# Mode parameters in two halves, low parts of the weights on VectorE, integers of phases on TensorE

## The chip, the cores and the metric

The kernel runs on one core of a Trainium2 chip. Its engines are TensorE (PE, with weight loads PEld), VectorE (DVE), ScalarE (ACT), GpSimd (POOL) and SyncE (SP), which issues nearly all the transfers. The metric is the device time of one execution in microseconds.

## The reference

A sequence `u` of 2048 positions and 448 channels goes through two branches, mixed by a gate for each position:

```python
g = _sigmoid((x * gate_w).sum(-1, keepdims=True))
a = _A_ref(x, ...)      # S4D convolution + skip
b = _B_ref(x, ...)      # (sigmoid(x W) * (x V)) W2, with 1792 inner features
return g * a + (1 - g) * b

# _A_ref: 448 channels, 256 modes each
A = -jnp.exp(log_A_real) + 1j * A_imag
C = (C_real + 1j * C_imag) * dt[:, None]
P = jnp.exp((A * dt[:, None])[:, :, None] * pos[None, None, :])
K = 2.0 * jnp.einsum("dn,dnl->dl", C, P).real
y = irfft(rfft(u_t, 2 * L) * rfft(K, 2 * L))[:, :, :L]
```

All is fp32.

## The kernel before

Four pieces of work share the engines.

- **Parameters** (`params`, tiles of the pool `pro`). From 448 x 256 mode parameters DVE, ACT and POOL make the phases of the modes in turns (each split into a high and a low part, `hi` and `lo`, stored to the DRAM tensor `phd`) and powers of their decays (`bsx`, stored to `bsd`). ACT takes exp, tanh, arctan and sin for it and loads a table at each change between these. The step size `dtv` is computed for 4 columns of 112 channels; its way to all 128 partitions (`dtb`) is a store to DRAM (`dtd`) and a load with broadcast.
- **Mode generation** (`kgen`, 28 chunks of 16 channels, 14 to each half of the channels). Chunk `c` loads its phases `ph` and powers `bs`, POOL multiplies the powers up to a table `tb` (`powers`), and for each half of the modes (`half_chunk`, so 56 of them) there are two calls of `turns`, each for 512 columns: PE multiplies phases with positions into PSUM (`tp`, L973), the integer is taken off, and ACT takes sine and cosine (`fr`, `ec`). DVE multiplies these with products of `tb` (`es`, `ec`: L1012, L1026, L1028, L1030, L1032; a half chunk has six such products), and PE sums over the modes into `kp` (L1038). After 14 chunks half of the convolution kernel K goes to the DRAM tensor `kd`.
- **Transforms** (`Chain`): `spectrum_u` for both halves of `u`, beside mode generation; then for each half the transform of K, the product with the spectrum of `u`, and the way back to the output. They need `kd`.
- **GLU** (`glu_w`, `glu_up`, `glu_down`, `glu_end`): 2 halves of the positions x 14 tiles of features. Each fp32 operand is split into a high part (`wh`, `vh`, `xs`, `hh`, cast by ACT) and a low part (`wl`, `vl`, `hl`, the difference), and each product is three fp32r matmuls: `gu` into 512 columns (L1142 to L1147), `dn` into 448 (L1159 to L1161). DVE does `sg`, `hl` and `ob` (L1131, L1134, L1175).

The integer of a phase comes off in one of two ways. In the half chunks that `PEM = (1, 2)` puts on PE, ACT rounds twice (L983 and L984, which leaves minus the integer in `nn`), PE repeats the product and adds `nn` by an identity matrix (L988), and ACT reads PSUM (L990, L991). In the others ACT rounds once (L978), DVE subtracts (L979), and ACT goes on from SBUF (L1002, L1003). With `(1, 2)` every second half chunk goes either way.

The low parts of the weights are computed in `glu_split`, L1118. Where the group (7 for each half of the positions) is under `GLO = 12` POOL does it, else DVE.

No order is written out. Every operation is recorded with its engine, a cost and a priority; `Plan.order` runs them through a model of the machine (`Clock`) and starts, on the engine that is free first, the ready operation of lowest priority number. `RANK` overwrites priorities by engine, tile and stage. The order found is fixed in the program, so each engine waits in that order. Buffers are counted per tile name (`tp` 2, `nn` 1, `kp` 1, `gu` 2, `dn` 1, `tb` 2), and a pool can be opened when the pools in its `after` have no work left: `eg` (mode generation) and `fu` (the first transforms) both follow `pro`, in which also the gate's and GLU's first inputs lie (`gt`, `xr0`).

Of the kernel before, what the change touches and what calls it, by code (L numbers as in the profile page):

```python
# [28 lines left out]
    ('Act', 'ec', 20): (-63, -6.5, 45, 54.5, 20, 20, 20, 20),  # L29
    ('Act', 'ex0', 10): -65.5,  # L30
    ('Act', 'fr', 20): (20, 20, 20, 20, 20, 41, -4.5, -4.5),
    ('Act', 'fx', 30): 110.5,
    ('Act', 'fx', 40): 91.5,
    ('Act', 'hh', 21): (21, 36, 36, 36, -17.5, 21),
    ('Act', 'hh', 45): 53.5,
    ('Act', 'ke', 20): -130.5,
    ('Act', 'nn', 20): (20, 20, 51, 51, 60, -97.5, 20, 20),
    ('Act', 'ob', 21): (-15.5, 21),
    ('Act', 'sg', 5): (5, 5, 125.5, 125.5, 5),
    ('Act', 'sg', 21): (21, 21, 68, 68, 68, -73.5),  # L40
    ('Act', 'sg', 45): 34.5,
    ('Act', 'th0', 10): -24,
    ('Act', 'vh', 5): -148,
    ('Act', 'vh', 21): (80, 61, 21),
    ('Act', 'wh', 5): -110,
    ('Act', 'wh', 21): (-131, 17, 21, 21, 21, 21),
    ('Act', 'xs', 5): -122.5,
    ('DVE', 'aci', 10): -43.5,
    ('DVE', 'dtp', 10): 0.5,
    ('DVE', 'dtv', 10): -76.5,  # L50
# [145 lines left out]
class Pool:  # L196
    def __init__(self, plan, name, space, after, below):
        self.plan, self.name, self.space, self.after, self.below = plan, name, space, after, below
        self.stack, self.tp = ExitStack(), None
# [9 lines left out]
    def real_pool(self):  # L209
        if self.tp is None:  # L210
            for p in self.after:
                p.stack.close()
            if self.below is not None:
                self.below.real_pool()
            self.tp = self.stack.enter_context(self.plan.tc.tile_pool(
                name=self.name, bufs=1, **({} if self.space is None else dict(space=self.space))))
# [1070 lines left out]
```

## Time and profile before

| | |
|---|---|
| time, median of 3 runs | 800.59 us (798.03 to 802.04) |
| profiled execution | 799.93 us, of which 797.8 us span |
| mean granted TensorE clock | 0.966 |
| busy: PE, DVE, ACT, POOL | 736.6, 714.9, 491.9, 342.0 us |
| HBM traffic | 74.39 MB read, 36.24 MB written, 139 GB/s over the span |

How to read a row of the groups: line, engine, operation, written tile `<-` read tiles, shapes, count | busy us, mean ns of one | idle time of the engine just before these instructions, and what ended most of it. Durations overlap a little: the next instruction of an engine can start before the last one's end, so prices are better taken from start to start. A timeline row begins with start and length in us. Matmuls overlap most.

### The profile page before, as it was taken

To read this page: it belongs to the slowest core of one execution; us is meant where nothing else is said; L and a number is where in the kernel's file an instruction comes from. 1 tells how busy PE (TensorE), PEld (TensorE's weight loads), DVE (VectorE), ACT (ScalarE), POOL (GpSimd) and SP (SyncE) were. 2 spreads that over 40 slices of the span, in tenths; PEclk is the share of its full clock that TensorE was granted. 3 is DMA by queue.
4 is the path that set the end of the run, shared out by engine and by line. 5 is a ranking of instruction groups with operands and counts; after the bars stand their busy time and mean duration, and the time that the engine had idled before them with its cause. 6 is when DMAs were issued, how large, how long until landed. Compare 5 with 4: busy or idle time off the path is not lost.

```text
span 797.8 us, 16605 instructions
## 1 busy us (share of the span) xinstructions
PE 736.6 (92%) x6688; PEld 526.8 (66%) x6688; DVE 714.9 (90%) x910; ACT 491.9 (62%) x818; POOL 342.0 (43%) x342
## 2 busy tenths in 40 slices
...
GB/s 284 195 108 70 175 191 202 149 185 200 74 115 185 136 117 210 166 242 139 170 137 183 239 71 12 43 12 51 30 73 256 209 38 99 117 109 131 204 102 173
DMA packets 97940, 111.71 MB, mean 140 GB/s; under 512 B 31272, under 2 KB 84840, under 8 KB 97352
## 3 DMA queue, kind: packets, MB, share of 16 engines
...
q8 instruction: 53, 0.87, 0.5%
q0 software_dynamic: 256, 0.46, 0.2%
...
HBM read 74.39 MB, written 36.24 MB: 139 GB/s over the span
## 4 chain that ended last, share of the span: by engine, by line
PE 47%; DVE 29%; ACT 7%; DMA 5%; issue 5%; POOL 3%; SPq 2%; DVEq 0%; ACTq 0%; POOLq 0%
PE gu_gps L1142 5%; PE gu_gps L1144 5%; PE gu_gps L1143 5%; PE kp_egp L1038 4%; PE dn_gps L1159 4%; PE fps_fups L617 4%; DVE ec_eg L1030 3%; PE dn_gps L1160 3%; DVE es_eg L1012 3%; PE dn_gps L1161 3%; PE tp_egp L973 3%; DVE es_eg L1032 2%; SPq L484 2%; DMA kd<-ke_eg 2%; DMA vr_glu<-in_w_dram 2%
## 5 line engine op out<-in xcount | busy, mean ns | idle before, releaser
L1142 PE MATMUL gu_gps<-xs_glu,wh_glu 128*128 128x512 f32 x336 | 141.2, 420 | 18.7 <-ACT wh_glu L1116 10.8
L1143 PE MATMUL gu_gps<-xs_glu,wh_glu 128*128 128x512 f32 x336 | 134.5, 400 | 0.0
L1144 PE MATMUL gu_gps<-xs_glu,wl_glu 128*128 128x512 f32 x336 | 134.2, 399 | 0.2 <-POOL wl_glu L1118 0.2
L1012 DVE TENSOR_TENSOR es_eg<-tb_eg 128x1024 f32<-128x1024 f32 (+1 forms) x112 | 118.1, 1079 | 2.8 <-PE kp_egp L1038 1.9
L1159 PE MATMUL dn_gps<-vh_glu,hh_glu 128*128 128x448 f32 x224 | 90.8, 405 | 7.5 <-DVE ob_glu L1175 4.3
L1142 PEld LDWEIGHTS gu_gps<-xs_glu,wh_glu 128*128 128x128 f32 x336 | 64.9, 193 | 40.8 <-ACT wh_glu L1116 10.8
L959 POOL TENSOR_TENSOR tb_eg<-tb_eg 128x96 f32<-128x96 f32 (+2 forms) x84 | 88.1, 1054 | 5.6
L1160 PE MATMUL dn_gps<-vh_glu,hl_glu 128*128 128x448 f32 x224 | 83.3, 372 | 4.3 <-DVE hl_glu L1134 4.3
L1161 PE MATMUL dn_gps<-vl_glu,hh_glu 128*128 128x448 f32 x224 | 82.9, 370 | 1.1 <-POOL vl_glu L1118 1.1
L1118 POOL TENSOR_TENSOR wl_glu<-xr_glu,wh_glu 128x512 fp32r<-128x512 f32 x44 | 73.2, 1676 | 24.9 <-ACT wh_glu L1116 24.9
L973 PE MATMUL tp_egp<-pos_sb,ph_eg 96*128 96x512 f32 x168 | 73.7, 458 | 9.3 <-DVE fr_eg L979 5.4
L1032 DVE TENSOR_TENSOR es_eg<-fr_eg,es_eg 128x1024 f32<-128x1024 f32 x56 | 81.7, 1459 | 0.1
L1118 POOL TENSOR_TENSOR vl_glu<-vr_glu,vh_glu 128x448 fp32r<-128x448 f32 x24 | 36.0, 1500 | 103.9 <-ACT vh_glu L1116 102.1
L1030 DVE TENSOR_TENSOR ec_eg<-ec_eg,es_eg 128x1024 f32<-128x1024 f32 x56 | 76.5, 1365 | 0.1
L1144 PEld LDWEIGHTS gu_gps<-xs_glu,wl_glu 128*128 128x128 f32 x336 | 64.8, 193 | 15.9 <-POOL wl_glu L1118 0.9
L1143 PEld LDWEIGHTS gu_gps<-xs_glu,wh_glu 128*128 128x128 f32 x336 | 65.1, 194 | 11.5 <-issue 0.4
L1130 ACT ACTIVATE sg_glu<-gu_gps 128x512 f32<-128x512 f32 x56 | 33.5, 598 | 55.4 <-PE gu_gps L1147 52.4
L949 POOL MEMSET tb_eg<- 128x96 f32 x28 | 7.8, 285 | 134.3 <-DVE es_eg L1012 133.5
L1005 ACT ACTIVATE ec_eg<-ec_eg,half_pi 128x1024 f32<-128x1024 f32 x56 | 64.5, 1151 | 0.5
L1159 PEld LDWEIGHTS dn_gps<-vh_glu,hh_glu 128*128 128x128 f32 x224 | 42.4, 189 | 31.1 <-issue 8.1
L1175 DVE SCALAR_TENSOR_TENSOR ob_glu<-dn_gps,og,ob_glu 128x448 f32<-128x448 f32 x72 | 48.5, 673 | 9.7 <-PE dn_gps L1161 9.2
L1133 ACT ACTIVATE hh_glu<-sg_glu 128x512 fp32r<-128x512 f32 x56 | 34.4, 629 | 36.8 <-DVE sg_glu L1131 33.4
...
## 6 DMA issues: line engine op xcount, KB each, us to landing
...
```

Of the source, the lines that this page charges most:

```text
L959: pool(96 * m, lambda n=n, m=m: G.tensor_mul(g3(n + 1, m), g3(1, m), g3(n, 1).to_broadcast([128, 32, 3, m])))
L973: T.matmul(tp.real, ph[:, c % 2, 128 * nh:128 * nh + 128].bitcast(F32R), pos[:, 512 * i:512 * i + 512], start=True, stop=last)
L1012: V.tensor_mul(o.rearrange("p d (i k) -> p d i k", k=ny), x.unsqueeze(3).to_broadcast([128, 16, nx, ny]), y.unsqueeze(2).to_broadcast([128 ...
L1030: op("DVE", c_dve(1024), lambda: V.tensor_mul(ec[:, :, 32:96], ec[:, :, 32:96], es[:, :, 32:96]), [(es, 1), (es, 2)], [(ec, "p")], prio)
L1032: op("DVE", c_dve(1024), lambda: V.tensor_mul(es[:, :, 32:96], fr.real, es[:, :, 32:96]), [fr], [(es, 1), (es, 2)], prio)
L1118: op(eng, cost(n), lambda: e.tensor_sub(view(l), a(), view(h).bitcast(F32)), [res, (h, key)], [(l, key)], prio)
L1142: T.matmul(p.real, wh[:, k, cs], x[:, k], start=(k == 0), stop=False)
L1143: T.matmul(p.real, wh[:, k, cs], x[:, 4 + k], start=False, stop=False)
L1144: T.matmul(p.real, wl[:, k, cs], x[:, k], start=False, stop=False)
L1159: T.matmul(p[:, :D], hh[:, ts], vh.real, start=(i == 0), stop=False)
L1160: T.matmul(p[:, :D], hl[:, ts], vh.real, start=False, stop=False)
L1161: T.matmul(p[:, :D], hh[:, ts], vl.real, start=False, stop=(i == len(fs) - 1))
```

## The change

- `params` runs once for each half of the channels (`g` = 0, 1), on half as many columns, with its own loads, stores and table loads. `phd` and `bsd` are tracked by half, so chunks 0 to 13 need the first half alone. The second half has the priority `P_PRO1 = 19`, one ahead of mode generation's 20.
- The step sizes are computed once (`step_sizes`). A diagonal matrix of them, multiplied on PE by a matrix of ones, spreads them over the partitions in PSUM; `dtd` is gone.
- `GLO = 0`: the low parts of all weights are computed on DVE. POOL did 24 of 28 tiles of features before (two `wl` and one `vl` each).
- `PEM = (1, 1)`: in all 56 half chunks the integer comes off on PE; L979, L978, L1002 and L1003 are no longer issued.
- The pool `pro` is divided: gate and first GLU inputs are in `pre` on one side of SBUF, and `eg` follows `pre` there; `pro` and after it `fu` lie on the other side.
- `RANK` is another table of priorities throughout.

```diff
-    ('DVE', 'wl', 45): 272,
+    ('DVE', 'wl', 21): 109.5,
+    ('DVE', 'wl', 45): 123,
...
-PEM = (1, 2)
-GLO = 12
+PEM = (1, 1)
+GLO = 0
...
-P_PRO, P_E, P_U, P_K, P_G, P_GV = 10, 20, 30, 40, 60, 21
+P_PRO, P_PRO1, P_E, P_U, P_K, P_G, P_GV = 10, 19, 20, 30, 40, 60, 21
...
-    pro, fups = plan.pool("pro"), plan.pool("fups", PSUM)
-    fu = plan.pool("fu", after=[pro])
-    eg, egp = plan.pool("eg", after=[pro], below=fu), plan.pool("egp", PSUM)
+    pre, fups = plan.pool("pre"), plan.pool("fups", PSUM)
+    pro = plan.pool("pro", side="right")
+    fu = plan.pool("fu", after=[pro], side="right")
+    eg, egp = plan.pool("eg", after=[pre]), plan.pool("egp", PSUM)
...
+        ones = pro.tile("ones", 1, (P, 128))
+        op("DVE", c_fast(128), lambda: V.memset(ones.real, 1.0), [], [ones], prio)
+        return dt2, dtp, dtv, ones
+
+    def params(g, sizes, prio):
+
+        dt2, dtp, dtv, ones = sizes
...
+        W, Q, cols, raw = 2 * N, D, slice(2 * g, 2 * g + 2), {}
...
-            for z, y in ((0, hi), (1, lo)):
-                dma(lambda z=z: phd[kind + z].rearrange("(t p) n -> p t n", p=P), lambda y=y: y.real.bitcast(F32),
-                    P * W * 4, [y], [(phd, kind + z)], prio)
-        dma(lambda: dtd.v("t p -> p t"), dtv, P * 16, [dtv.res], [dtd], prio, 0.35)
...
+        diag, dtb = pro.tile("diag", 1, (P, 2, P)), fups.tile("fps", FPS, (128, 512))
+        for i in range(2):
+            op("DVE", c_fast(P), lambda i=i: V.tensor_scalar(
+                diag[:, i], idn[0:P, 0:P].bitcast(F32), dtv()[:, 2 * g + i:2 * g + i + 1], None, op0=ALU.mult),
+               [idn, dtv.res], [(diag, i)], prio)
+        op("PE", c_mm4(HD), lambda: T.matmul(dtb[:, :HD], ones.real, diag.v("p t q -> p (t q)"), start=True, stop=True),
+           [ones, diag], [dtb], prio)
...
                 dma(lambda i=i: ph[:, i], lambda i=i: phd[:, 16 * (c + i):16 * (c + i) + 16], 96 * 1024,
-                    [phd], [(ph, i)], prio, 115.0)
+                    [(phd, (k, c // 14)) for k in range(6)], [(ph, i)], prio, 115.0)
...
-    params(P_PRO)
+    sizes = step_sizes(P_PRO)
+    params(0, sizes, P_PRO)
     gate(2, P_G2)
     gate(3, P_G2)
+    params(1, sizes, P_PRO1)
     kgen_consts(P_E)
```

What the new priorities make of the order shows at three places. Line numbers after the change are higher by 31 or 32 for the same statement (L1012 becomes L1043, L1118 becomes L1150).

First, DVE at the start of mode generation: before, from the last parameter operation (`bsx`) to the first product `es`.

```order
L893 TENSOR_TENSOR bsx_pro_971<-th_pro_807,ex_pro_802 128x2x14x32
L1175 SCALAR_TENSOR_TENSOR ob_glu_624<-dn_gps_962,og,ob_glu_624 128x448
L1131 SCALAR_TENSOR_TENSOR sg_glu_954<-sg_glu_954,gu_gps_950 128x512
L1134 TENSOR_TENSOR hl_glu_1006<-sg_glu_898,hh_glu_996 128x512
L1175 SCALAR_TENSOR_TENSOR ob_glu_678<-dn_gps_983,og,ob_glu_678 128x448
L1134 TENSOR_TENSOR hl_glu_1026<-sg_glu_954,hh_glu_1000 128x512
L1131 SCALAR_TENSOR_TENSOR sg_glu_1046<-sg_glu_1046,gu_gps_1040 128x512
L1134 TENSOR_TENSOR hl_glu_1089<-sg_glu_1046,hh_glu_1082 128x512
L1012 TENSOR_TENSOR es_eg_1138<-tb_eg_1055 128x16x64
```

And after, up to the first `es`:

```order
L924 TENSOR_TENSOR bsx_pro_1260<-th_pro_1178,ex_pro_1189 128x2x7x32
L834 TENSOR_TENSOR lo_pro_1266<-acr_pro_761,hi_pro_1228 112x512
L1150 TENSOR_TENSOR wl_glu_1272<-xr_glu_826,wh_glu_1244 128x512
L1150 TENSOR_TENSOR wl_glu_1272<-xr_glu_885,wh_glu_1244 128x512
L1150 TENSOR_TENSOR vl_glu_1313<-vr_glu_1255,vh_glu_1304 128x448
L1163 SCALAR_TENSOR_TENSOR sg_glu_1284<-sg_glu_1284,gu_gps_1276 128x512
L1150 TENSOR_TENSOR wl_glu_1334<-xr_glu_888,wh_glu_1315 128x512
L1207 SCALAR_TENSOR_TENSOR ob_glu_491<-dn_gps_1166,og,ob_glu_491 128x448
L1150 TENSOR_TENSOR wl_glu_1334<-xr_glu_1195,wh_glu_1315 128x512
L834 TENSOR_TENSOR lo_pro_1353<-mx_pro_820,hi_pro_1292 112x512
L1043 TENSOR_TENSOR es_eg_1379<-tb_eg_1274 128x16x64
```

The parameters' operations (here the second half's) now reach up to the first `es`, and low parts of weights stand among them: 22 `wl` and 8 `vl` are ahead of the first `es` on DVE, 24 and 12 between it and the last one, 10 and 8 behind.

Second, DVE within the first chunk: before, from the middle of the first half chunk to the end of the second.

```order
L1030 TENSOR_TENSOR ec_eg_1160<-ec_eg_1160,es_eg_1138 128x16x64
L1175 SCALAR_TENSOR_TENSOR ob_glu_467<-dn_gps_1202,og,ob_glu_467 128x448
L979 SCALAR_TENSOR_TENSOR fr_eg_1190<-fr_eg_1190,tp_egp_1212 128x512
L1028 SCALAR_TENSOR_TENSOR es_eg_1138<-fr_eg_1119,es_eg_1138 128x16x32
L1032 TENSOR_TENSOR es_eg_1138<-fr_eg_1119,es_eg_1138 128x16x64
L1026 TENSOR_TENSOR ec_eg_1265<-ec_eg_1265,es_eg_1171 128x16x32
L1030 TENSOR_TENSOR ec_eg_1265<-ec_eg_1265,es_eg_1171 128x16x64
```

After, the same stretch:

```order
L1061 TENSOR_TENSOR ec_eg_1370<-ec_eg_1370,es_eg_1379 128x16x64
L1059 SCALAR_TENSOR_TENSOR es_eg_1379<-fr_eg_1332,es_eg_1379 128x16x32
L1063 TENSOR_TENSOR es_eg_1379<-fr_eg_1332,es_eg_1379 128x16x64
L1166 TENSOR_TENSOR hl_glu_1491<-sg_glu_1146,hh_glu_1479 128x512
L1057 TENSOR_TENSOR ec_eg_1443<-ec_eg_1443,es_eg_1403 128x16x32
L1166 TENSOR_TENSOR hl_glu_1529<-sg_glu_1215,hh_glu_1517 128x512
L1207 SCALAR_TENSOR_TENSOR ob_glu_561<-dn_gps_1450,og,ob_glu_561 128x448
L1166 TENSOR_TENSOR hl_glu_1541<-sg_glu_1284,hh_glu_1531 128x512
L1061 TENSOR_TENSOR ec_eg_1443<-ec_eg_1443,es_eg_1403 128x16x64
```

The subtraction L979, which stood between the products, is gone; GLU's operations still stand there.

Third, PE in the first chunk: before, the first product of the second half chunk (`tp_egp_1179`, whose integer DVE subtracts, as it does that of `tp_egp_1212` above), and the end of the first half chunk's second call of `turns` (`tp_egp_1115`).

```order
L973 MATMUL tp_egp_1179<-pos_sb,ph_eg_1034 128x512
L973 MATMUL tp_egp_1115<-pos_sb,ph_eg_1034 128x512
L988 MATMUL tp_egp_1115<-nn_eg_1173,idn 128x512
L1142 MATMUL gu_gps_1162<-xs_glu_166,wh_glu_720 128x512
L1143 MATMUL gu_gps_1162<-xs_glu_166,wh_glu_720 128x512
```

After, the ends of the two calls of `turns` for the second half chunk (`tp_egp_1387` and `tp_egp_1399`).

```order
L1004 MATMUL tp_egp_1387<-pos_sb,ph_eg_1223 128x512
L1019 MATMUL tp_egp_1387<-nn_eg_1413,idn 128x512
L1174 MATMUL gu_gps_1394<-xs_glu_115,wh_glu_1170 128x512
L1175 MATMUL gu_gps_1394<-xs_glu_115,wh_glu_1170 128x512
L1176 MATMUL gu_gps_1394<-xs_glu_115,wl_glu_1186 128x512
L1174 MATMUL gu_gps_1394<-xs_glu_115,wh_glu_1170 128x512
L1175 MATMUL gu_gps_1394<-xs_glu_115,wh_glu_1170 128x512
L1176 MATMUL gu_gps_1394<-xs_glu_115,wl_glu_1186 128x512
L1004 MATMUL tp_egp_1399<-pos_sb,ph_eg_1223 128x512
L1019 MATMUL tp_egp_1399<-nn_eg_1436,idn 128x512
L1191 MATMUL dn_gps_1450<-vh_glu_1099,hh_glu_1106 128x448
```

The pair of a repeated `tp` and its `nn` now comes for every call of `turns`: 224 + 112 matmuls into `tp` in place of 168 + 56. Between the first and the last `kp` PE has 555 `gu` and 312 `dn` in place of 611 and 324, and behind the last `kp` 305 and 210 in place of 302 and 210. SP issues 31 transfers for the parameters in place of 18.

More of the change, by code (lines that the diff above doesn't have):

```diff
@@ L28 @@
 RANK = {
[L29 to L50, printed above, removed]
[23 rows of a table removed]
-    ('DVE', 'uax', 40): (-66, 40),
-    ('DVE', 'ubx', 40): 55,
[31 rows of a table removed]
+    ('Act', 'acr', 10): 271,
+    ('Act', 'ci', 10): 33,
+    ('Act', 'cr', 10): 123.5,
+    ('Act', 'dots', 2): 39,
+    ('Act', 'ec', 20): (20, -161.5, 24.5, 24.5, 20, -7, -7, 30),
+    ('Act', 'ex0', 10): -38,
+    ('Act', 'ex1', 10): 195.5,
+    ('Act', 'fr', 20): (20, 20, 20, 20, 38.5, 38.5, 31, 31),
+    ('Act', 'fx', 30): 168.5,
+    ('Act', 'fx', 40): (40, 40, 40, -20, -20, -20, -20, -20),
+    ('Act', 'hh', 21): -5,
+    ('Act', 'hh', 45): 167.5,
+    ('Act', 'ke', 20): (89.5, 89.5, 20, -26.5, 20, -19.5, 20, 20),
+    ('Act', 'nn', 20): (-125, -125, -125, -6, 20, -179, 31, 20),
+    ('Act', 'ob', 5): 153,
+    ('Act', 'ob', 21): -110.5,
+    ('Act', 'rt', 19): 47.5,
+    ('Act', 'sg', 5): (5, 13, 198, 198, 5),
+    ('Act', 'sg', 21): (21, 21, 21, 174.5, 174.5, 174.5),
+    ('Act', 'sg', 45): 55.5,
+    ('Act', 'th1', 10): 105.5,
+    ('Act', 'th1', 19): -42,
+    ('Act', 'vh', 21): (21, 145.5, -19.5),
+    ('Act', 'vh', 45): -108,
+    ('Act', 'wh', 21): (-35, -35, -35, 111, 111, 111),
+    ('Act', 'wh', 45): 84,
+    ('DVE', 'acr', 19): 116.5,
[29 rows of a table added]
+    ('DVE', 'uax', 40): -207,
+    ('DVE', 'ubx', 40): 226.5,
[33 rows of a table added]
 }
@@ L212, in real_pool @@
                 p.stack.close()
[L213 to L216, printed above, removed]
+            kw = {} if self.space is None else dict(space=self.space)
+            if self.side is not None:
+                kw["side"] = self.side
+            self.tp = self.stack.enter_context(self.plan.tc.tile_pool(name=self.name, bufs=1, **kw))
         return self.tp
@@ L299, in __init__, with pool @@
         self.tc, self.ops = tc, []
-    def pool(self, name, space=None, after=(), below=None):
-        return Pool(self, name, space, after, below)
+    def pool(self, name, space=None, after=(), side=None):
+        return Pool(self, name, space, after, side)
     def op(self, eng, cost, fn, r=(), w=(), prio=0, after=(), size=0, table=None):
@@ new lines, in gated_mix, with __init__, __call__, rw @@
+    class A:
+        def __init__(self, res, f=lambda r: r):
+            self.res, self.f = res, f
+        def __call__(self):
+            return self.f(self.res.real)
+    def rw(o, *ins):
+        return [x.res for x in ins], [o.res]
+    P = 112
+    steps, POW = (64.0, 1.0, 512.0, 8.0), (2, 0, 3, 1)
+    class Params:
+        def __init__(self, prio):
+            self.prio = prio
+        def ts(self, o, a, s1, s2, o0, o1=None, n=2 * N):
+            kw = dict(op0=o0) if o1 is None else dict(op0=o0, op1=o1)
+            op("DVE", c_fast(n), lambda: V.tensor_scalar(o(), a(), s1, s2, **kw), *rw(o, a), self.prio)
+        def stt(self, o, a, s, b, o0, o1, n=2 * N):
+            op("DVE", c_dve(n), lambda: V.scalar_tensor_tensor(o(), a(), s, b(), op0=o0, op1=o1), *rw(o, a, b), self.prio)
+        def tt(self, o, a, b, o0, n=2 * N):
+            op("DVE", c_dve(n), lambda: V.tensor_tensor(o(), a(), b(), op=o0), *rw(o, a, b), self.prio)
+        def act(self, o, a, fn, n=2 * N, table=None, **kw):
+            op("Act", c_act(n), lambda: S.activation(o(), a(), fn, **kw), *rw(o, a), self.prio, table=table)
+        def mk(self, name, w=(2, N), dt=F32, rows=P):
+            return A(pro.tile(name, 1, (rows, *w), dt))
@@ L874, in params @@
         split(mx, 2)
-        bsx = pro.tile("bsx0", 1, (128, 14, 2, 32))
-        for nh in halves:
-            amp_t(cr, idn, bsx, nh, prio)
-        bs_store(bsx, 4, prio)
+        bsx = pro.tile("bsx0", 1, (128, 7, 2, 32))
+        for nh in range(2):
+            amp_t(cr, bsx, nh, prio)
+        bs_store(bsx, 4, g, prio)
         for i in range(4):
```

136 lines of the change are left out of this document (59 added, 77 removed), and 113 rows, old and new, of the table RANK.

## The prediction

> **What bounds the kernel now.** I read the page's engine shares first, then the chain, then the same busy times cut into the three stages of the program.
>
> ```profile
> PE 736.6 (92%) x6688; PEld 526.8 (66%) x6688; DVE 714.9 (90%) x910; ACT 491.9 (62%) x818; POOL 342.0 (43%) x342
> ...
> PE 47%; DVE 29%; ACT 7%; DMA 5%; issue 5%; POOL 3%; SPq 2%; DVEq 0%; ACTq 0%; POOLq 0%
> ```
>
> TensorE (PE) and VectorE (DVE) are both full, and the chain of work that ended last changes between them. The stages are cut at the first `es` product (129.3 us, timeline below) and at the last one, which starts at 584.75 and lasts 1.23.
>
> ```profile
> 0.00:129.30 129.30, 105.99 (x440) 85.19 (x441) 104.28 (x143) 68.98 (x107) 65.41 (x51) 0.96 0.67 171
> 129.30:586.00 456.70, 430.17 (x5200) 309.46 (x5198) 437.06 (x490) 369.59 (x614) 269.49 (x286) 0.96 0.46 130
> 586.00:797.80 211.80, 200.45 (x1058) 132.13 (x1050) 173.60 (x279) 53.37 (x97) 7.14 (x6) 0.99 0.55 142
> ```
>
> Columns: stretch, length, then busy PE, PEld, DVE, ACT, POOL, granted clock, DMA. In stage 2 (mode generation with GLU work between) DVE is busy 437.1 of 456.7 us, 95.7%; PE 94%. But a busy PE has slack that busy time does not show:
>
> ```profile
> 559.00 0.50 PE L973 MATMUL tp_egp<-pos_sb,ph_eg 96*128 96x512 f32 x1
> 559.34 0.40 PE L1146 MATMUL gu_gps<-xs_glu,wh_glu 128*128 128x512 f32 x1
> 559.58 0.39 PE L1147 MATMUL gu_gps<-xs_glu,wl_glu 128*128 128x512 f32 x1
> ```
>
> A matmul of 512 columns counts 0.40 busy, yet the next starts 0.24 later, and 0.34 behind the one of 96 rows; a `dn` of 448 columns I take at 0.2. So DVE bounds stage 2, with PE close behind.
>
> **The parts, stage by stage.** Counts come from the two programs' orders, durations from this execution.
>
> *Stage 3 first.* Behind the last mode product PE has 302 `gu` and 210 `dn` matmuls left before the change, 305 and 210 after, and the same transforms. DVE gets 2 `wl` and 4 `vl` more, some 3.3 us where it is busy 82%. I take +1, so everything hangs on when stage 2 ends.
>
> *Low parts from POOL to DVE.*
>
> ```profile
> L1118 POOL TENSOR_TENSOR wl_glu<-xr_glu,wh_glu 128x512 fp32r<-128x512 f32 x44 | 73.2, 1676 | 24.9 <-ACT wh_glu L1116 24.9
> L1118 POOL TENSOR_TENSOR vl_glu<-vr_glu,vh_glu 128x448 fp32r<-128x448 f32 x24 | 36.0, 1500 | 103.9 <-ACT vh_glu L1116 102.1
> L1118 DVE TENSOR_TENSOR wl_glu<-xr_glu,wh_glu 128x512 fp32r<-128x512 f32 x8 | 5.4, 691 | 0.1
> L1118 DVE TENSOR_TENSOR vl_glu<-vr_glu,vh_glu 128x448 fp32r<-128x448 f32 x4 | 2.5, 614 | 0.0
> 558.26 0.69 DVE L979 SCALAR_TENSOR_TENSOR fr_eg<-fr_eg,tp_egp 128x512 f32<-128x512 f32 x1
> 558.87 0.68 DVE L1028 SCALAR_TENSOR_TENSOR es_eg<-fr_eg,es_eg 128x512 f32<-128x512 f32 x1
> 579.32 1.21 DVE L1030 TENSOR_TENSOR ec_eg<-ec_eg,es_eg 128x1024 f32<-128x1024 f32 x1
> 580.45 0.67 DVE L1175 SCALAR_TENSOR_TENSOR ob_glu<-dn_gps,og,ob_glu 128x448 f32<-128x448 f32 x1
> ```
>
> The last four rows are neighbours in the timeline: a DVE operation of 512 elements takes 0.61 from start to start, one of 1024 takes 1.13, so 1.0 ns an element and 0.08 fixed. A `wl` is 0.61, a `vl` of 448 about 0.54. Stage 1 gets 22 and 8 of them (17.7 us), stage 2 gets 24 and 12 (21.1 us). What queues behind them on DVE are the mode products, for which PE waits.
>
> *Integers taken off on TensorE.* The 56 operations of L979 go from DVE: 56 x 0.61 = 34.2 us, all in stage 2. They also stood in a loop with two waits, which go with them; their place is taken by the loop over `nn`, which half of the chunks have already:
>
> ```profile
> ACT ec_eg L1002 <- DVE fr_eg L979: 21.9, 16, 4.3
> DVE ec_eg L1026 <- ACT ec_eg L1005: 11.0, 12, 3.1
> PEld tp_egp L973 <- DVE fr_eg L979: 9.3, 13, 3.5
> PEld tp_egp L988 <- ACT nn_eg L984: 5.5, 11, 1.5
> ```
>
> (engine, line, whom it waited for: us in total, times, longest.) The `nn` wait doubles, +5.5; up to 9.3 goes. I cost the two as nothing; the cover is GLU matmuls standing between, and in 460 to 540 us, where these are few, the wait is bare.
>
> PE gains 56 repeated L973 and 56 L988. In stage 2 that is 109 matmuls, 26 us by 0.24 or 37 by 0.34; out of stage 2 into stage 1 go 56 `gu` and 12 `dn`, 15.8 us; 8 transform matmuls come in, 2 us. Net +12 to +23; I take 12, since most of the added ones follow a neighbour of 128 rows.
>
> ACT gets, for each of 28 half chunks, twice (L983, L984, L990, L991) instead of twice L978, L1002 and L1003:
>
> ```profile
> L984 ACT ACTIVATE nn_eg<-fr_eg 128x512 fp32r<-128x512 f32 x56 | 35.6, 637 | 0.1
> L991 ACT ACTIVATE fr_eg<-tp_egp 128x512 f32<-128x512 f32 x56 | 33.7, 601 | 11.2 <-PE tp_egp L988 10.9
> L990 ACT ACTIVATE ec_eg<-tp_egp 128x512 f32<-128x512 f32 x56 | 33.6, 601 | 6.1 <-PE tp_egp L988 6.0
> L978 ACT ACTIVATE fr_eg<-tp_egp 128x512 f32<-128x512 f32 x56 | 32.1, 610 | 8.8 <-DVE es_eg L1032 8.8
> L983 ACT ACTIVATE fr_eg<-tp_egp 128x512 f32<-128x512 f32 x56 | 30.7, 591 | 3.7 <-DVE es_eg L1032 1.8 <-PE tp_egp L973 1.3 <-DMA ph_eg<-phd 0.3
> L1002 ACT ACTIVATE ec_eg<-fr_eg 128x1024 f32<-128x1024 f32 x28 | 29.7, 1060 | 22.2 <-DVE fr_eg L979 21.9
> L1003 ACT ACTIVATE fr_eg<-fr_eg 128x1024 f32<-128x1024 f32 x28 | 29.5, 1053 | 0.3
> ```
>
> That is 4.86 against 3.33 us: +43 us on 369.6, less 5 for nine GLU casts and sigmoids that went to stage 1. It stays under a 436 us stage (94% at most, since neighbours overlap): costed at nothing, covered by DVE and PE. If those got faster still, ACT would be next.
>
> *Contention between POOL and DVE.*
>
> ```profile
> L1032 DVE TENSOR_TENSOR es_eg<-fr_eg,es_eg x56: 1208/1220/2332, 143.9 to 584.8; 128x1024 f32<-128x1024 f32 x56
> L1032 DVE TENSOR_TENSOR es_eg<-fr_eg,es_eg 128x1024 f32<-128x1024 f32 x56 | 81.7, 1459 | 0.1
> L1030 DVE TENSOR_TENSOR ec_eg<-ec_eg,es_eg 128x1024 f32<-128x1024 f32 x56 | 76.5, 1365 | 0.1
> L979 DVE SCALAR_TENSOR_TENSOR fr_eg<-fr_eg,tp_egp 128x512 f32<-128x512 f32 x56 | 37.7, 678 | 2.3 <-ACT fr_eg L978 2.0
> 129.30:586.00 456.70, 0.00 (x0) 71.37 (x43) 0.96 0.46 130
> 129.30:586.00 456.70, 118.08 (x112) 200.23 (x243) 0.96 0.46 130
> ```
>
> L1032 takes 1220 in the median but 1459 in the mean; L1030 1365. Against 1220 that is 13.4 and 8.1 us, and the whole stretch lies between these 21.5 and about 50 over all products on SBUF operands. L979, which reads PSUM, is not stretched (678). The last two rows are POOL's busy time in stage 2 on L1118 and on `tb`: 71.4 and 200.2. By that share, 26% of 50, the low parts' leaving gives 13 us. Ends: 0, if `tb` meets the same products anyway, and 50. I take 13, the share that the rows show.
>
> [...]
>
> *Stage 2's sum.* DVE: 437.1 - 34.2 + 21.1 - 2.4 (three `sg`, one `ob` fewer) - 13 = 408.6; at the same 95.7% the stage would last 427. PE: 430.2 + 12 = 442 busy. In the last 46 us before 586 both engines are full at once (45.70 and 45.93):
>
> ```profile
> 460.00:540.00 80.00, 68.19 (x865) 48.64 (x864) 77.00 (x82) 63.01 (x101) 51.50 (x56) 0.87 0.11 31
> 540.00:586.00 46.00, 45.70 (x547) 35.11 (x545) 45.93 (x53) 31.36 (x49) 17.63 (x15) 1.00 0.11 36
> ```
>
> So neither has to give way, but PE cannot go far under 442/0.99 = 446 except by the 0.17 us tails that fill gaps. Between 427 and 446 I take 436: -21 us.
>
> *Halves and step sizes, stage 1.*
>
> ```profile
> 116.51 1.08 DVE L893 TENSOR_TENSOR bsx_pro<-th_pro,ex_pro 128x896 f32<-128x896 f32 x1
> ...
> 126.32 0.69 DVE L1131 SCALAR_TENSOR_TENSOR sg_glu<-sg_glu,gu_gps 128x512 f32<-128x512 f32 x1 [3.55 <-PE gu_gps L1147]
> ...
> 129.29 1.88 DVE L1012 TENSOR_TENSOR es_eg<-tb_eg 128x1024 f32<-128x1024 f32 x1 [0.77 <-POOL tb_eg L959]
> ...
> 0.00:129.30 129.30, 0.00 (x0) 35.76 (x23) 0.96 0.67 171
> ...
> L832 ACT ACT_TABLE_LOAD x2 | 2.6, 1283 | 0.0
> ```
>
> (The row with 35.76 is POOL's busy time on L1118 in stage 1.) Parameters end at 117.6; store, load and powers take until 129.3, and DVE stands idle for some 6 of these 11.7 us, 3.55 in one piece. After the change the second half of the parameters fills that gap, since the loads for chunk 0 need the first half alone. But in the order every one of the second half's DVE rows still stands before the first `es`, with 30 low parts: halving moves no parameter work behind the start. DVE: 104.3 + 17.7 + 3 (35 split operations by 0.08) + 2.4 (three `sg`, one `ob`) = 127.4, less a relief at stage 2's price for POOL's time, 13/71.4 of 35.8: 6.5 (ends 0 and 25, from 0 and 50 there). The idle 25 falls by the gap's 6 at least; I take 8 for it. Sum 121 + 17 = 138, of which I keep 137: +8. It isn't lost: 53 `gu` and 12 `dn` have been done by then. ACT's six more table loads, 1.28 us each, are covered by its idle 60 us. SP's 13 more parameter transfers move the same bytes: nothing, between 0 and the gap's 6. The step sizes' trip through DRAM goes, one matmul per half comes: nothing, since `la` then waits for DVE's own queue.
>
> [...]
>
> **Sum.** 137 + 436 + 213 = 786 of span against 797.8; the execution took 799.93, 2.1 more, and lies 0.08% under the median of 800.59. I predict 788.
>
> **Rivals.** *PE bounds (slower).* PE keeps the waits that it has, at 94% busy, and the 109 added matmuls come on top at 0.34 in place of 0.24: stage 2 becomes 456.7 + 23 = 480, or 469 at the low price; with +8 and +1 the run takes 832 or 821, less what the waits for L979 gave (9.3), so 812 at the least. Against: 12 of PE's 26.5 idle us lie in 460 to 540, where DVE is 96% busy. It decides from the point where stage 2 needs over 448 us. 812.
>
> *Traded evenly.* No relief from POOL, and products wait for ACT's longer loop (the 11.0 us of L1026 double): DVE 421.6 + 11 and 456.7 - 437.1 idle give 452, or 441 without the doubled wait; with 137 + 213 + 2 that is 804 or 793, in the middle 799.
>
> *More comes.* Relief 26, twice its share, and both engines full: DVE 396/0.97 = 408, PE at its 0.24 pitch not in the way; stage 1 unchanged. 129 + 408 + 213 + 2 = 752 at most; half of the way from the forecast, 770.
>
> **How the numbers follow.** The forecast has 0.5, more comes 0.2, traded evenly 0.17, PE bounds 0.13. Within 0.5% means within 4 us of 800.6, about what a measurement tells from no change. Faster holds the first two: 0.70; same 0.17; slower 0.13. The range cuts the lower half of "more comes" and the upper half of "PE bounds": 771 to 812. The forecast's own range is 779 to 796.
>
> **What would show it.** Right: first `es` at 135 to 139, last one at 565 to 580; DVE busy in between near 409; means of the two 1024-element products under 1400; POOL near 230 in all; the waits for L979 gone. Wrong: PE over 97% busy in stage 2 with DVE under 90%; products waiting for ACT above 20 us; a first `es` before 125, if parameters by halves start the modes early after all; or a stage 3 off 212 by over 4.

## The result, and the profile after

The changed kernel takes 778.32 us (median of 4 runs, 777.54 to 781.98) against 800.58 us (798.03 to 802.04) in runs on the same chip: a ratio of 0.9734, 95% interval 0.9695 to 0.9774, so 22 us less. The profiled execution after has a span of 776.4 us.

The page's engine shares and granted clock after:

```profile
PE 743.2 (96%) x6804; PEld 539.9 (70%) x6804; DVE 687.8 (89%) x967; ACT 527.3 (68%) x962; POOL 230.4 (30%) x282
...
PEclk9999999999999999999999999999999999999999
```

PE works 6.6 us more than before, and the span is 21.4 shorter: PE's idle time fell from 61.2 to 33.2 us. The windows say where, cut as before at the first and the last `es` product (length, then busy PE, PEld, DVE, ACT, POOL, granted clock, DMA):

```profile
0.00:136.20 136.20, 119.79 (x519) 97.98 (x520) 114.50 (x218) 87.90 (x154) 39.41 (x46) 0.99 0.62 168
136.20:560.30 424.10, 419.84 (x5234) 307.68 (x5233) 397.36 (x467) 386.77 (x712) 190.94 (x237) 1.00 0.52 138
560.30:776.40 216.10, 203.53 (x1054) 134.25 (x1053) 175.97 (x285) 52.62 (x97) 0.00 (x0) 0.99 0.54 139
```

Against 129.3, 456.7 and 211.8: stage 1 is 6.9 longer, stage 2 32.6 shorter, stage 3 4.3 longer. PE's idle time in stage 2 went from 26.5 to 4.3 us, and the stretch 460 to 540, where PE had worked 68.19 of 80 at a clock of 0.87, is full:

```profile
460.00:540.00 80.00, 79.84 (x928) 61.16 (x928) 76.63 (x91) 71.64 (x130) 34.02 (x45) 1.00 0.15 49
```

The groups of DVE's products and of its new low parts:

```profile
L1063 DVE TENSOR_TENSOR es_eg<-fr_eg,es_eg 128x1024 f32<-128x1024 f32 x56 | 72.6, 1297 | 0.1
L1061 DVE TENSOR_TENSOR ec_eg<-ec_eg,es_eg 128x1024 f32<-128x1024 f32 x56 | 71.2, 1272 | 0.5
L1043 DVE TENSOR_TENSOR es_eg<-tb_eg 128x1024 f32<-128x1024 f32 x56 | 69.7, 1245 | 10.2 <-PE kp_egp L1069 6.0 <-POOL tb_eg L993 1.6 <-POOL tb_eg L990 1.3
L1150 DVE TENSOR_TENSOR wl_glu<-xr_glu,wh_glu 128x512 fp32r<-128x512 f32 x52 | 37.1, 735 | 1.2 <-ACT wh_glu L1148 1.2
```

The means of the first two were 1459 and 1365. The waits that the prediction spoke of (whole span: us, times, longest):

```profile
ACT ec_eg L1021 <- PE tp_egp L1019: 15.1, 19, 3.9
DVE ec_eg L1057 <- ACT ec_eg L1036: 12.1, 13, 2.9
DVE vl_glu L1150 <- ACT vh_glu L1148: 12.0, 5, 5.1
PEld tp_egp L1019 <- ACT nn_eg L1015: 2.4, 8, 0.8
```

Those for L979 are gone. The wait of PE's weight loads for `nn`, expected to double from 5.5, fell to 2.4; a matmul of GLU now stands right in front of 73 of the 112 repeated products (29 of 56 before). New is DVE's wait for the cast `vh`.

### The profile page after: what moved, and what is told of

Its sections match the earlier page's. It is cut to its first block, busy times and chain, and to the rows that moved or that the text cites. A ratio compares the mean times of both kernels' runs of the same rounds, so it can differ in the third digit from the quotient of the medians.

```text
span 776.4 us, 17036 instructions
## 1 busy us (share of the span) xinstructions
PE 743.2 (96%) x6804; PEld 539.9 (70%) x6804; DVE 687.8 (89%) x967; ACT 527.3 (68%) x962; POOL 230.4 (30%) x282
## 5 line engine op out<-in xcount | busy, mean ns | idle before, releaser
L1174 PE MATMUL gu_gps<-xs_glu,wh_glu 128*128 128x512 f32 x336 | 136.3, 406 | 11.2 <-ACT wh_glu L1148 10.8
L1175 PE MATMUL gu_gps<-xs_glu,wh_glu 128*128 128x512 f32 x336 | 132.6, 394 | 0.0
L1043 DVE TENSOR_TENSOR es_eg<-tb_eg 128x1024 f32<-128x1024 f32 x112 | 107.8, 987 | 10.2 <-PE kp_egp L1069 6.0
L1004 PE MATMUL tp_egp<-pos_sb,ph_eg 96*128 96x512 f32 x224 | 97.1, 440 | 0.6 <-ACT fr_eg L1014 0.6
L990 POOL TENSOR_TENSOR tb_eg<-tb_eg 128x96 f32<-128x96 f32 (+2 forms) x84 | 84.1, 1005 | 6.2
L1021 ACT ACTIVATE ec_eg<-tp_egp 128x512 f32<-128x512 f32 x112 | 69.6, 622 | 16.1 <-PE tp_egp L1019 15.1
L1015 ACT ACTIVATE nn_eg<-fr_eg 128x512 fp32r<-128x512 f32 x112 | 74.8, 668 | 6.8 <-PE tp_egp L1019 6.7
L1063 DVE TENSOR_TENSOR es_eg<-fr_eg,es_eg 128x1024 f32<-128x1024 f32 x56 | 72.6, 1297 | 0.1
L1061 DVE TENSOR_TENSOR ec_eg<-ec_eg,es_eg 128x1024 f32<-128x1024 f32 x56 | 71.2, 1272 | 0.5
L1022 ACT ACTIVATE fr_eg<-tp_egp 128x512 f32<-128x512 f32 x112 | 69.2, 621 | 3.4 <-PE tp_egp L1019 3.3
L1014 ACT ACTIVATE fr_eg<-tp_egp 128x512 f32<-128x512 f32 x112 | 65.3, 626 | 3.6 <-DVE es_eg L1063 2.2
L993 POOL TENSOR_TENSOR tb_eg<-tb_eg,bs_eg 128x32 f32<-128x32 f32 x84 | 60.8, 726 | 6.2
```

The lines of the kernel that those rows point to most:

```text
L990: pool(96 * m, lambda n=n, m=m: G.tensor_mul(g3(n + 1, m), g3(1, m), g3(n, 1).to_broadcast([128, 32, 3, m])))
L1004: T.matmul(tp.real, ph[:, c % 2, 128 * nh:128 * nh + 128].bitcast(F32R), pos[:, 512 * i:512 * i + 512], start=True, stop=last)
L1015: op("Act", c_act(512), lambda: S.activation(nn.real, fi(), AF.Copy, scale=-1.0, bias=MAGIC), [(fr, i)], [nn], prio)
L1043: V.tensor_mul(o.rearrange("p d (i k) -> p d i k", k=ny), x.unsqueeze(3).to_broadcast([128, 16, nx, ny]), y.unsqueeze(2).to_broadcast([128 ...
L1061: op("DVE", c_dve(1024), lambda: V.tensor_mul(ec[:, :, 32:96], ec[:, :, 32:96], es[:, :, 32:96]), [(es, 1), (es, 2)], [(ec, "p")], prio)
L1063: op("DVE", c_dve(1024), lambda: V.tensor_mul(es[:, :, 32:96], fr.real, es[:, :, 32:96]), [fr], [(es, 1), (es, 2)], prio)
```

## The experiments

My theory: DVE's queue in mode generation set the length, and the change shortened it, by the subtractions that left and by the stretch that POOL's low parts had given to the products. Rivals: the order in the new `RANK` did it, not the parts; TensorE's granted clock did it (0.96 to 1.00 in stage 2). Each verdict is a ratio to the kernel before in runs on the same chip (medians of before 800.6 to 802.7); microseconds between two kernels are the difference of their ratios times 800.6.

| kernel | median us | ratio, 95% interval |
|---|---|---|
| after | 778.32 | 0.9734, 0.9695 to 0.9774 |
| e1: after, integers back, planned anew | 829.62 | 1.0318, 1.0260 to 1.0376 |
| e2: after, low parts back, planned anew | 799.67 | 0.9957, 0.9926 to 0.9988 |
| e3: before with integers alone | 798.74 | 0.9945, 0.9919 to 0.9971 |
| e4: before with low parts alone | 821.25 | 1.0225, 1.0158 to 1.0293 |
| e6: before, L979 cut short | 788.34 | 0.9830, 0.9801 to 0.9858 |
| e7: before, POOL's low parts as memsets | 784.61 | 0.9802, 0.9762 to 0.9842 |
| e8: after's order, low parts back | 803.55 | 1.0015, 0.9992 to 1.0037 |
| e9: after's order, integers back | 798.43 | 0.9960, 0.9934 to 0.9985 |
| e10: after, no `RANK` | 796.00 | 0.9921, 0.9893 to 0.9948 |
| e11: before, no `RANK` | 822.50 | 1.0243, 1.0209 to 1.0277 |
| e5: before with both, no halves, no `RANK` | 815.83 | 1.0173, 1.0103 to 1.0244 |
| e12: after, repeated products cut short | 773.21 | 0.9633, 0.9606 to 0.9661 |

### One part at a time, planned anew (e1 to e4)

In these the planner makes a new order from the table that it has (priorities of operations that a variant lacks are skipped).

```diff
 e1: -PEM = (1, 1)   +PEM = (1, 2)      in after
 e2: -GLO = 0        +GLO = 12          in after
 e3: -PEM = (1, 2)   +PEM = (1, 1)      in before
 e4: -GLO = 12       +GLO = 0           in before
```

> After, with PEM = (1, 2): in every second half chunk DVE subtracts the integer again (56 of L979's kind), halves and low parts as after. The planner then sends 55 gu and 51 dn fewer through mode generation and leaves 55 gu and 48 dn more behind it. Theory (DVE's load is what fell): DVE gets 34 us back in mode generation, less 8 for GLU operations that left; about 24 us slower than after, 795 to 808. Rival 1 (the order is what counts, DVE's load is not): as after with only the moved GLU work, 774 to 784. Rival 2 (TensorE's clock): slower only as far as TensorE stands idle and its granted clock in mode generation falls back under 0.98.

> After, with GLO = 12: POOL computes 24 of 28 tiles' low parts again, halves and integers as after. Mode generation starts earlier (32 rows fewer on DVE ahead of it). Theory (POOL's work stretches DVE's products about as much as DVE's own low parts cost): DVE in mode generation 397 - 21 + 24, even; the start 5 to 8 earlier; 768 to 782. Rival 1 (by the count alone): 39 us less DVE work, 745 to 765, and then TensorE would be the bound. Rival 2 (contention costs more than the count): 785 to 800, with means of the two 1024-element products back at 1360 to 1460.

> Before, with PEM = (1, 1): integers of all half chunks on TensorE, parameters whole and POOL's low parts as before. Theory: DVE 437 - 34 = 403 in mode generation, TensorE 430 + 12 = 442 busy with less idle; 780 to 790. Rival 1 (TensorE bounds, its waits stay): 800 to 815. Rival 2 (the tuned order is what brought the gain): 798 to 812, since this order's priorities were not made for it.

> Before, with GLO = 0: all low parts on DVE, integers and parameters as before. 16 wl and 7 vl come ahead of the modes, 30 and 13 between them. Theory (relief about even with the load): start of the modes 3 to 8 later, DVE in mode generation 437 + 25 - 24; 798 to 812, products' means near 1270 and 1300. Rival (no relief): 437 + 25 and +13 at the start, 825 to 840.

Stages 2 and 3 of e1, stage 2 of e3, stages 1 and 3 of e4 (windows):

```profile
136.30:568.60 432.30, 395.62 (x5020) 281.46 (x5019) 414.52 (x510) 357.11 (x592) 206.12 (x237) 0.93 0.51 135
568.60:825.10 256.50, 232.91 (x1156) 155.28 (x1154) 185.15 (x298) 58.54 (x105) 0.00 (x0) 0.95 0.47 119
```

```profile
130.90:581.60 450.70, 445.00 (x5335) 325.35 (x5333) 418.54 (x437) 399.07 (x730) 258.69 (x288) 1.00 0.47 132
```

```profile
0.00:134.00 134.00, 100.53 (x413) 81.44 (x414) 105.41 (x162) 66.70 (x104) 32.99 (x36) 0.92 0.64 165
587.30:814.50 227.20, 197.12 (x1008) 127.91 (x1006) 173.37 (x282) 52.45 (x96) 0.00 (x0) 0.93 0.50 132
```

All four missed the theory's numbers on the slow side. e2 lost 18 us to after and lies in rival 2's range, with the two products' means at 1476 and 1386 ns, about where this rival had put them (1360 to 1460); the next runs bear it out. In e1 stage 2 is 8 us longer than after's, but stage 3 is 40 longer. The 55 `gu` and 48 `dn` put behind account for some 23 of the 40 by the prediction's 0.24 and 0.2 each; the rest, of which 11 is idle time of PE, stays open. e3 gained 4 where I had said 10 to 20: PE is busy 445 of 450.7 us, for this order has 613 `gu` and 345 `dn` between the first and the last `kp` where after has 555 and 312. e4 lost 18 where I had said at most 11. Its profiled execution is 16.7 us longer than before's: stage 1 takes 4.7 more, stage 2 3.4 less, and stage 3 15.4 more. So the loss lies at the end, where PE idles 30.1 us in place of 11.4, with 272 `gu` and 195 `dn` left behind the last `kp` in place of 302 and 210. A part taken alone with an order that was not made for it thus measures the order too. The next runs keep the order.

### One part taken back in an unchanged order (e8, e9)

Here after's order is planned as it is, and only at issue an operation is replaced.

```diff
 e8, in glu_split:
+run = G if group < 12 else V
-op(eng, cost(n), lambda: e.tensor_sub(view(l), a(), view(h).bitcast(F32)), ...)
+op(eng, cost(n), lambda: run.tensor_sub(view(l), a(), view(h).bitcast(F32)), ...)
 e9, in turns, for every second half chunk:
-S.activation(nn.real, fi(), AF.Copy, scale=-1.0, bias=MAGIC)
+V.scalar_tensor_tensor(fi(), fi(), MAGIC, tp.real, op0=ALU.subtract, op1=ALU.subtract)
-x(False); T.matmul(tp.real, idn.real, nn.real, start=False, stop=True)
-S.activation(..., tv(), AF.Abs);  S.activation(..., tv(), AF.Sin, scale=TWO_PI)
+S.activation(..., fr[:, ds], AF.Abs);  S.activation(..., fr[:, ds], AF.Sin, scale=-TWO_PI)
```

> After, with the order that was planned for after, but the low parts of 24 of 28 tiles issued on POOL at the same places: against e2_low_back only the order of the rest differs. Theory (POOL's stretch costs what DVE's share saves, and e2's loss of 21 us lies in its order): 772 to 784. Rival 1 (the low parts on POOL cost by themselves, through stretch and by coming later): 790 to 802. Rival 2 (DVE's count alone): 750 to 765.

> After, with the order planned for after, but in every second half chunk DVE subtracts the integer at the place where ACT made nn, and the repeated product and the nn matmul are not issued: 56 DVE operations more (34 us), 112 matmuls and 56 ACT operations fewer. Against e1_integer_back the GLU work stays where it was. Theory (DVE's load): mode generation 424 becomes 440 to 455, 794 to 810. Rival 1 (TensorE is the bound now and gets 26 us back): 755 to 776. Rival 2 (the two cancel, and e1's 51 us are its order): 774 to 786.

Stages 1 and 2 of e8, and its groups of two products, of the gate's products `gt` and of `sg`, which reads PSUM:

```profile
0.00:144.80 144.80, 121.27 (x516) 98.39 (x517) 116.04 (x188) 87.06 (x153) 78.70 (x69) 0.96 0.58 156
144.80:583.50 438.70, 423.93 (x5236) 307.54 (x5236) 403.47 (x431) 389.35 (x713) 245.93 (x280) 1.00 0.51 134
```

```profile
L1063 DVE TENSOR_TENSOR es_eg<-fr_eg,es_eg 128x1024 f32<-128x1024 f32 x56 | 77.6, 1386 | 0.1
L1061 DVE TENSOR_TENSOR ec_eg<-ec_eg,es_eg 128x1024 f32<-128x1024 f32 x56 | 76.9, 1373 | 0.5
L1164 DVE SCALAR_TENSOR_TENSOR sg_glu<-sg_glu,gu_gps 128x512 f32<-128x512 f32 x56 | 38.0, 681 | 9.7 <-PE gu_gps L1180 9.3
L730 DVE SCALAR_TENSOR_TENSOR gt_pre<-gt_pre,gwb_pre 128x448 f32<-128x448 f32 x16 | 12.9, 820 | 0.0
```

The same last two groups of after:

```profile
L1163 DVE SCALAR_TENSOR_TENSOR sg_glu<-sg_glu,gu_gps 128x512 f32<-128x512 f32 x56 | 38.2, 684 | 5.5 <-PE gu_gps L1179 4.2 <-ACT acr_pro L887 0.8
L730 DVE SCALAR_TENSOR_TENSOR gt_pre<-gt_pre,gwb_pre 128x448 f32<-128x448 f32 x16 | 11.0, 700 | 0.0
```

Rival 1 holds, with 22 us of loss to after. In e8 DVE issues 36 low parts fewer in stage 2, 21.1 us by the prediction's prices, and yet is busy 6.1 us longer than after: POOL's low parts stretch the rest by 27 us. In stage 1 it issues 30 fewer, 17.7 us, and is busy 1.5 longer: 19 us of stretch, and the first `es` comes 8.6 later. `gt`, which reads SBUF alone, is stretched (700 to 820 ns), and so are the two products (1297 to 1386 and 1272 to 1373); `sg`, which reads PSUM, is not (684 to 681). Of rival 1's two ways, coming later has little part in it: all of PE's waits for POOL's low parts come to 2.1 us (1.7 for `vl`, 0.4 for `wl`).

e9 loses 18 us, as the theory had it. Its stage 2, and the waits of PE and its weight loads for DVE's products from 136 to 560 us, then the same of after:

```profile
133.20:578.00 444.80, 402.05 (x5122) 289.12 (x5121) 425.54 (x523) 372.24 (x656) 194.47 (x237) 0.99 0.50 132
```

```profile
PE kp_egp L1087 <- DVE ec_eg L1079: 13.2, 19, 1.4
PE kp_egp L1087 <- DVE es_eg L1081: 12.0, 18, 1.8
...
PEld kp_egp L1087 <- DVE es_eg L1081: 24.8, 35, 1.9
```

```profile
PE kp_egp L1069 <- DVE ec_eg L1061: 0.3, 2, 0.2
...
PEld kp_egp L1069 <- DVE es_eg L1063: 6.6, 19, 0.4
```

DVE gets 28.2 us more work, PE 17.8 less, and stage 2 grows by 20.7: what PE no longer does it spends waiting for products. That is DVE's queue as the cause. The two losses, 18 and 22 us, add up to more than the 22 of the whole change, so the parts are not additive; no run takes both back in this order. e1 lost 29 us more than e9 with the same parts, so that much came with e1's order (and with the lower clock that it ran at, 0.93 in its stage 2 against 0.99). The clock is not the cause of after's gain: e9's stage 2 has 0.99, e8's and e3's 1.00, and they take 445, 439 and 451 us, while e6 and e7, next, gain at 0.97.

### One load taken away in before's order (e6, e7)

```diff
 e6:
-op("Act", ..., lambda: S.activation(fi(), tp.real, AF.Copy, bias=MAGIC), ...)
+op("Act", ..., lambda: S.activation(fi(), tp.real, AF.Copy, scale=1e-6), ...)
-fi(), fi(), MAGIC, tp.real, op0=ALU.subtract, op1=ALU.subtract)
+fi()[:, 0:8], fi()[:, 0:8], 0.0, tp[:, 0:8], op0=ALU.mult, op1=ALU.mult)
 e7, where POOL computes a low part:
-e.tensor_sub(view(l), a(), view(h).bitcast(F32))
+G.memset(view(l).bitcast(F32), 0.0)
```

> Before, in its own order, with L979 cut from 512 columns to 8 (the integer is then not taken off in those half chunks): DVE gets 56 x 0.53 = 30 us less in mode generation, nothing else changes. Theory (DVE's load sets mode generation's length): 20 to 30 less, 772 to 784. Rival (the order and TensorE's work set it, DVE's load is covered): 793 to 802.

> Before, in its own order, with each low part that POOL computes replaced by a memset to 0 of the same tile (the low parts of 24 of 28 tiles are then left out): no POOL operation with two SBUF inputs but those of tb. Theory (POOL's low parts stretch DVE's products by 24 us): products' means 1250 to 1300 in place of 1365 and 1459, 780 to 792. Rival 1 (the stretch is tb's alone): means as before, 797 to 803. Rival 2 (the stretch lies beside waits and frees nothing): means fall, 796 to 803.

Stage 2 of e6 and its L1032; stages 1 and 2 of e7, its L1032 and L1030:

```profile
130.60:574.70 444.10, 421.28 (x5181) 306.50 (x5183) 418.41 (x490) 370.35 (x614) 265.30 (x286) 0.97 0.48 134
```

```profile
L1032 DVE TENSOR_TENSOR es_eg<-fr_eg,es_eg 128x1024 f32<-128x1024 f32 x56 | 84.4, 1507 | 0.1
```

```profile
0.00:125.20 125.20, 102.79 (x437) 82.70 (x438) 94.47 (x143) 68.53 (x107) 40.00 (x52) 0.99 0.71 176
125.20:568.10 442.90, 423.94 (x5204) 307.48 (x5202) 408.01 (x491) 369.61 (x614) 207.59 (x285) 0.97 0.48 134
```

```profile
L1032 DVE TENSOR_TENSOR es_eg<-fr_eg,es_eg 128x1024 f32<-128x1024 f32 x56 | 72.8, 1301 | 0.1
L1030 DVE TENSOR_TENSOR ec_eg<-ec_eg,es_eg 128x1024 f32<-128x1024 f32 x56 | 72.1, 1287 | 0.1
```

Both loads are real and neither is worth its count. e6 gains 14 us (theory 20 to 30, so it missed at the low end): DVE's busy time fell by 18.7 and not 30, partly because its six products per half chunk took 7.2 us more in all (L1032 1459 to 1507). That they met POOL's work more often would explain it, but was not shown. e7 gains 16 us, as the theory had it: DVE's busy time falls by 29.1 us in stage 2 and by 9.8 in stage 1 though it issues the same operations; the stage falls by 13.8, the start comes 4.1 earlier. In both runs about half to two thirds of what DVE was spared in stage 2 reached the end (12.6 of 18.7, 13.8 of 29.1).

In e7 memsets of the same tiles in the same places leave the products at 1301 and 1287 ns, about as low as after's 1297 and 1272 without them. But a memset differs from the subtraction in two ways, it reads no tile and it is shorter (a `wl` takes 530 ns in place of 1676), so the run does not tell which of the two spares DVE:

```profile
L1118 POOL MEMSET wl_glu<- 128x512 f32 x48 | 24.3, 530 | 65.6 <-PE gu_gps L1148 65.6
```

### The parts without the table (e11, e5, e10)

```diff
 e10, e11, e5:
-for key, x in RANK.items():
+for key, x in ():
 e5, in before:
-PEM = (1, 2)   GLO = 12
+PEM = (1, 1)   GLO = 0
```

> Before, with the table RANK not applied. 810 to 870. Theory (the parts carry the gain): 20 to 30 more than e10. Rival (the table does): as much as e10.

> Before, with integers on TensorE and all low parts on DVE, parameters whole, and RANK not applied: what e10 has beyond it is the halves and the step sizes on TensorE. Theory (halves bring little, since both halves' rows stand ahead of the first product in after's order): within 6 of e10. Rival 1 (the halves fill the gap of 6 to 12 us at the end of the parameters): 6 to 15 more than e10. Rival 2 (the halves cost, 3 us of split operations and six table loads): 3 to 8 less than e10.

> After, with the table RANK not applied: the planner orders everything by the statements' own priorities. Together with e11 and e5_no_halves_plain_order it tells what the parts do in orders that nobody fitted to them. Theory (the parts carry the 22 us): 20 to 30 less than e11. Rival (the table carries them): within 8 of e11 or slower. In microseconds, with an order that is not fitted: 790 to 850.

The three windows of e5, then of e10:

```profile
0.00:153.90 153.90, 134.79 (x592) 111.28 (x593) 114.22 (x189) 77.66 (x123) 33.89 (x33) 0.99 0.64 156
153.90:598.00 444.10, 439.80 (x5305) 323.04 (x5304) 404.25 (x478) 397.23 (x729) 178.88 (x238) 1.00 0.48 134
598.00:815.30 217.30, 175.08 (x906) 108.75 (x904) 160.91 (x262) 42.77 (x78) 0.00 (x0) 0.92 0.50 131
```

```profile
0.00:116.70 116.70, 103.86 (x457) 86.72 (x458) 98.20 (x193) 76.22 (x133) 33.20 (x42) 1.00 0.65 168
116.70:574.70 458.00, 446.89 (x5327) 327.09 (x5325) 416.46 (x495) 403.00 (x738) 188.85 (x240) 0.99 0.51 135
574.70:798.30 223.60, 204.13 (x1024) 129.17 (x1022) 174.56 (x282) 51.36 (x94) 0.00 (x0) 0.95 0.52 135
```

The parts carry the gain without any fitted table: e10 takes 26 us less than e11 (0.9921 against 1.0243). So the rival that the new table alone did it falls; the two tables are worth 19 us (before) and 15 (after). But inside the 26 my theory was wrong: integers and low parts together give 6 (e11 to e5, intervals that overlap), and the halves, with the step sizes on TensorE and the divided pool, give 20, beyond all three ranges that I had written down. No run separates these three. The windows suggest how. Without halves the modes start at 153.9, and by the first `kp` PE has done so much GLU work (418 `gu`) that behind the last one only 217 `gu` and 150 `dn` are left beside the last transforms: it idles 42 us in stage 3. With halves the modes start at 116.7, after 336 `gu` at the first `kp`, while DVE still works on the second half's parameters:

```profile
115.51 0.69 DVE L766 SCALAR_TENSOR_TENSOR mx_pro<-mx_pro,rt_pro 112x512 f32<-112x512 f32 x1
116.12 0.68 DVE L769 TENSOR_TENSOR cr_pro<-cr_pro,acr_pro 112x512 f32<-112x512 f32 x1
116.73 1.21 DVE L1043 TENSOR_TENSOR es_eg<-tb_eg 128x1024 f32<-128x1024 f32 x1
```

Stage 2 gets 14 us longer for it, and stage 3, with 294 `gu` and 192 `dn`, is 6 longer but has PE idle for 19.5 only. Over the whole span PE's idle time falls from 65.6 to 43.4 us. What the halves are worth in the fitted order was not measured apart: there the first `es` stands behind the second half's parameters.

### Is TensorE the bound now? (e12)

```diff
-x(False); T.matmul(tp.real, idn.real, nn.real, start=False, stop=True)
+T.matmul(tp[:, 0:16], ..., pos[:, 512 * i:512 * i + 16], start=True, stop=False)
+T.matmul(tp[:, 0:16], idn.real, nn[:, 0:16], start=False, stop=True)
 (and the two activations behind with scale=1e-6)
```

> After, in its own order, with the repeated product and the nn matmul cut from 512 columns to 16 (the integer is then taken off in 16 columns alone): TensorE gets 224 x some 0.2 = 45 us less in mode generation, all else stays. Theory (TensorE, 99% busy there, is the bound of after): 424 falls until DVE's 397 of work stops it, to 400 to 412, so 752 to 766. Rival (DVE and the waits between the two set it; TensorE's busy time has slack): 772 to 780.

Stage 2, a piece of the timeline, and DVE's two longest waits in stage 2:

```profile
134.20:556.20 422.00, 404.57 (x5233) 300.46 (x5232) 394.83 (x467) 386.13 (x712) 195.38 (x237) 0.99 0.52 139
```

```profile
303.68 0.28 PE L1018 MATMUL tp_egp<-pos_sb,ph_eg 96*128 96x16 f32 x1
303.81 0.26 PE L1020 MATMUL tp_egp<-nn_eg,idn 128*128 128x16 f32 x1
303.92 0.48 PE L1175 MATMUL gu_gps<-xs_glu,wh_glu 128*128 128x512 f32 x1
```

```profile
DVE ec_eg L1058 <- ACT ec_eg L1037: 11.6, 13, 2.7
DVE es_eg L1044 <- PE kp_egp L1070: 6.6, 8, 1.8
```

Close to the rival. By this piece a cut pair takes 0.24 us from its first start to the next matmul's, in place of some 0.48 by the prediction's pitch, so 112 pairs spare PE some 27 us in all, less than the 45 that I had put down; its busy time in stage 2 fell by 15.3, and stage 2 by 2.1 (profiled span 3.3, by the ratios 8). PE is busy 99% of after's stage 2, and yet PE alone does not bound it. DVE's share is 93.6%, as after. The largest part of DVE's idle 27.2 us is its wait for ACT (11.6, and 12.1 in after), which is busy 91% of the stage in both; the wait for PE is 6.6 (6.0 in after). No run takes work off ACT, so whether ACT's loop or the hand-over between PE and DVE sets the length now stays open.

## Why the prediction came out as it did

Forecast 788, range 771 to 812; 778 came. That is just under the forecast's own 779 to 796 and about as near to the 770 of "more comes" as to 788. The direction and the path were right; two terms of stage 2's sum were mis-sized, and both made the gain too small. Of the signs, the first `es` (136.2), the products' means, POOL's 230 and the end of the waits for L979 held. DVE's 397 us and the last `es` at 559.0 lie below the stated 409 and 565 to 580.

- **Stage 1, 137: 136.2.** Right, by two errors that cancel. DVE is busy 114.5, not 121: the relief from POOL is 13, where I took 6.5. Its idle time fell by 3.3 (25.0 to 21.7), not 8; 4.3 of what is left is the new wait of `vl` for `vh`.
- **Contention, -13: the step that failed.** I split the stretch by POOL's busy time, 26% for L1118. The rows of after say otherwise: above 1220 ns the two products kept 4.3 and 2.9 us of their 13.4 and 8.1, so two thirds went. e8 and e7 measure the whole: 27 and 29 us, twice my 13. The sharing rule was wrong: a microsecond of low parts (448 and 512 elements) disturbs DVE more than one of `tb`'s small operations (32 to 288). By these two products, an estimate, it is 0.20 us of stretch (14.3 us went with the 71.4 of L1118) against 0.04 (7.2 stayed beside the 190.9 of `tb` in after). Why was not tried. DVE came to 397, not 409.
- **PE, 442 busy: 419.8.** By e9, the same stage with the old split of integers is 402 of PE work and not the 430.2 - 15.8 + 2 = 416 of my count, and the 112 matmuls add 17.8, not 26. Of the first gap of 14, some 5 is the count: by the traces, stage 2 of e9 has 66 `gu` and 8 `dn` fewer than before's (not 56 and 12) and as many transform matmuls, some 18.5 us in place of 13.8. The other 9 is a busy time per matmul that is 2.3% shorter. Before's granted clock of 0.96 against 0.99 would give 416 x 0.03 = 12, an estimate; that the clock is the cause is not shown. So PE did not stop the stage at 446.
- **Between the two ends, 436: 424.1.** With the measured loads, the same rule has 415 for DVE (397.4/0.957) and 424 for PE (419.8/0.99). The stage came at the upper end: DVE's share fell from 95.7% to 93.7%, so part of its relief turned into waiting.
- **L979, -34.2, its waits as nothing: right in kind, a little too large.** In the unchanged order it is 28 us of DVE's busy time and 18 us of the run (e9). The wait for `nn`, which was to double, fell to 2.4.
- **ACT, +38, hidden: right in kind.** It is 386.8, 17 more, at 91% of the shorter stage; products wait 12.1 us for it (11.0 before).
- **Stage 3, +1: 216.1, +4.3.** Wrong by the limit that I had set. PE is busy 3.1 us more there and idle 1.2 more. DVE's new `vl` wait, 7.8 us in this stage, is hardly the reason: in e8, with low parts on POOL, it is 1.0 and the stage takes 218.7. What is, stays open.
- **The halves.** That they move no parameter work behind the start holds for after's order. That they are worth only a gap of 8 us is a reading of that order, not of the edit: without the table they were worth 20, together with the step sizes on TensorE and the divided pool.

Of the rivals, "more comes" had the relief (26; 27 measured) and PE full, but not DVE full: 93.7%, not 97%, and 424 in place of 408. "PE bounds" fell, with the added matmuls going into time in which PE had stood idle (26.5 us of stage 2 before, 4.3 after). The sign that would have spoken for it came by half: PE over 97% busy in stage 2 (99%), but DVE not under 90%. "Traded evenly" fell with its doubled wait (12.1).
